# Row sums of the attention weights: four accumulating DMAs and a VectorE reduce for 28 heads, in place of a ones matmul for every two or four heads

## The chip, the cores and the metric

The kernel runs on one core of a Trainium2 chip. The core has five engines that work side by side: TensorE (PE in the profile) multiplies matrices, VectorE (DVE) and ScalarE (ACT) work on elements, GpSimd (POOL) and SyncE (SP) here mostly issue DMAs. An engine takes its instructions strictly in order, so an instruction that waits holds all that stand behind it on that engine. Transfers run on 16 DMA engines that all queues share. Accumulating DMAs, which add what they carry to what lies at the destination, are issued from POOL; most others from SP.

The metric is the device time of one execution in microseconds; of several executions the median counts.

## The reference: what is computed

```python
def _A_ref(x, wqkv, wo):                      # attention: B=1, S=2048, D=1024, H=32 heads, Dh=32
    qkv = (x @ wqkv).reshape(B, S, 3, H, Dh).transpose(2, 0, 3, 1, 4)
    q, k, v = qkv[0], qkv[1], qkv[2]
    scores = jnp.einsum("bhqd,bhkd->bhqk", q, k) * (Dh ** -0.5)
    p = _softmax(scores, axis=-1)
    o = jnp.einsum("bhqk,bhkd->bhqd", p, v)
    return o.transpose(0, 2, 1, 3).reshape(B, S, D) @ wo
...
g = _sigmoid((x * gate_w).sum(-1, keepdims=True))
a = _A_ref(x, A_wqkv, A_wo)
b = _B_ref(x, B_w_q, B_k1, B_k2, B_u, B_v)    # experts chosen by product keys
return g * a + (1 - g) * b
```

All of it is in 32-bit floats. The change concerns one quantity: for each head and each of the 2048 queries, the sum of exp(score) over the 2048 keys, by which the softmax divides.

## The kernel before

The kernel has three stages. The first projects x to queries and keys, routes to the experts and computes the values, and leaves its results in device memory. The second, from about 628 to 1625 us of the profile, is the attention of 32 heads. The third multiplies by wo, adds the experts' part and stores the output. The change lies in the second stage, apart from one constant tile that is set up at the start.

**Steps.** The attention is cut into 512 steps, 32 heads by 16 key tiles of 128 keys; step 16 h + kt is key tile kt of head h. For each step `scores` (line 1272) multiplies a key tile with all 2048 queries in four units of 512 queries. Each unit fills one bank of `ring`, seven banks of PSUM that are used in turn, and ScalarE takes the exponential of one to four banks at once (line 1294) into a tile P[h, kt] of 128 keys x 2048 queries. `pv` (line 1299) multiplies P with the values; a head's output gathers in the tile `o`, which ScalarE copies to `osb` when the head is done (`finish`, line 1407). Units come in batches of 8 to 10, and a batch's activations are cut where a key tile ends, where the ring wraps around, and after each of the first units of a batch longer than the ring.

**Row sums.** A head's 16 tiles P are added up to one tile of 128 x 2048 in two ways. In `PAIRS` stand pairs of tiles that an accumulating DMA of POOL adds into one, (0, 2), (4, 6) and (8, 10) for all heads but the last (`accumulate`, line 1335, at steps 4, 8 and 12 of the head). VectorE adds the other ten tiles into the head's accumulator ACC[h] as they come (`presum`, line 1323), and the sums of the pairs at steps 12, 17 and 21 of the head, counted on into the next head (`add_pair`, `merge4` and the like). `add` (line 1344) is two VectorE instructions of 128 x 1024.

What is left is a sum over the 128 partitions, which VectorE can't form, and so TensorE does it: with a matrix of ones, `head_sums` (line 1400) multiplies a tile into one bank of the ring, ScalarE copies the bank to `ssb` (line 1417), and SP stores the rows to SMD. To need one such matmul for four heads rather than four, the kernel folds each head of the first 24 from 128 partitions to 32 and puts it into its quarter of a shared tile T (`merge4`, `fold4`, `fold4_end`: two accumulating DMAs for the first head of four, three for the others, and for these an add of 32 partitions more on VectorE). The matrix `ones4` keeps the four quarters apart. Heads 24 to 29 are folded to 64 partitions and taken two at a time with `ones2`; heads 30 and 31 are taken alone. T lies in `rb0`, which the third stage needs for its first factors (`load_rb` from step 495 on).

For each group of four heads `load_r` then loads the sums as 128 x 64, and `norm_r` (line 1427) takes the reciprocal, multiplies it with the gate in G64 and stores it to RD, from which the third stage loads its factors.

**What sets the order.** Everything is written out by hand. `at(step, f, ...)` (line 1475) puts a call on a list for a step; the loop at line 1542 emits a batch of scores, the multiplications with values that lag behind it, and then for each finished step its listed calls and its `presum`. Each call lands at that place in the queues of the engines that it uses.

**Buffers.** `p_tile` (line 1158) chooses the place of each new P among 13 places, 11 from step 328 on and 10 from step 443 on, as the one that is free first by a fixed plan: a tile of a pair is planned for 14 or 10 steps, any other for 5. The accumulators come from two buffers named `acc` that are used in turn.

## Time and profile before

| | |
|---|---|
| median of three timed runs | 1811.02 us (1810.2 to 1812.05) |
| the profiled execution's own time | 1811.52 us |
| its span, first to last instruction | 1809.7 us |
| TensorE busy, matmuls | 1801.0 us |
| VectorE busy | 1503.6 us |
| ScalarE busy | 1221.5 us |
| GpSimd busy | 262.4 us |
| granted TensorE clock | 1.00 |

The profile is of one execution. Its page gives the busy time of each engine, the span in 40 slices (a digit is the busy share in tenths), the chain of work that ended last followed back from the end, and groups of instructions: source line, engine, operation, what is written and read, shape, count, then busy time, mean duration in nanoseconds and the idle time of the engine before them with what ended it. Matmuls overlap, so that a busy TensorE isn't TensorE at its peak, and the mean of one matmul is longer than its share of the busy time. A multiplication of plain 32-bit floats shows as two matmul records. A view by windows gives each engine's busy time in a stretch with the number of its instructions, the clock, the DMA share and the rate in GB/s.

### The profile page before, as it was taken

To read this page: it belongs to the slowest core of one execution; us is meant where nothing else is said; L and a number is where in the kernel's file an instruction comes from. 1 tells how busy PE (TensorE), PEld (TensorE's weight loads), DVE (VectorE), ACT (ScalarE), POOL (GpSimd) and SP (SyncE) were. 2 spreads that over 40 slices of the span, in tenths; PEclk is the share of its full clock that TensorE was granted. 3 is DMA by queue.
4 is the path that set the end of the run, shared out by engine and by line. 5 is a ranking of instruction groups with operands and counts; after the bars stand their busy time and mean duration, and the time that the engine had idled before them with its cause. 6 is when DMAs were issued, how large, how long until landed. Compare 5 with 4: busy or idle time off the path is not lost.

```text
span 1809.7 us, 28079 instructions
## 1 busy us (share of the span) xinstructions
PE 1801.0 (100%) x10631; PEld 1137.0 (63%) x10631; DVE 1503.6 (83%) x1673; ACT 1221.5 (67%) x1613; POOL 262.4 (15%) x314
## 2 busy tenths in 40 slices
PE   9999999999999999999999999999999999999999
PEld 7877777788888745555454555454555545547887
DVE  7868776358988689999989999999899989995674
ACT  4434321211233399999999999999999999993221
POOL 0212000026401211111211111111112010101000
PEclk9999999999999999999999999999999999999999
DMA  6887888723238699999999999999999998957851
GB/s 234 243 284 248 272 267 295 258 79 106 82 129 276 225 217 185 195 198 199 191 202 205 208 209 194 206 184 208 200 202 198 207 199 189 201 130 228 280 168 58
DMA packets 132225, 364.74 MB, mean 202 GB/s; under 512 B 17540, under 2 KB 57876, under 8 KB 106168
## 3 DMA queue, kind: packets, MB, share of 16 engines
q0 software_dynamic: 22064, 136.07, 39.3%
q1 hardware_dynamic: 89864, 190.94, 35.3%
q10 hardware_dynamic: 20160, 35.92, 7.0%
q8 instruction: 84, 1.38, 0.3%
q14 instruction: 53, 0.43, 0.1%
HBM read 169.14 MB, written 72.10 MB: 133 GB/s over the span
## 4 chain that ended last, share of the span: by engine, by line
PE 97%; DMA 2%; ACT 0%; issue 0%; DVE 0%; SPq 0%; ACTq 0%; DVEq 0%
PE ring L1285 29%; PE o L1306 26%; PE bk L157 13%; PE bk L713 10%; PE pa L157 6%; PE bk L760 5%; PE bk L928 2%; PE bk L313 2%; PE pa L1582 2%; PE bk L493 1%; PE bk L397 1%; PE pa L1589 1%; DMA wraw<-in_wqkv 1%; DMA smd<-ssb 1%; PE ring L1319 0%; ACT P L1294 0%
## 5 line engine op out<-in xcount | busy, mean ns | idle before, releaser
L1294 ACT ACTIVATE P<-ring 128x512 f32<-128x512 f32 (+3 forms) x995 | 807.8, 932 | 12.9 <-PE ring L1285 6.7
L1347 DVE TENSOR_TENSOR acc<-acc,P 128x1024 f32<-128x1024 f32 x516 | 596.0, 1219 | 30.5 <-ACT P L1294 29.8
L1306 PE MATMUL o<-P,V 128*32 128x512 f32 (+1 forms) x3896 | 408.7, 540 | 0.0
L1285 PE MATMUL ring<-Q,K 98*128 98x512 f32 x1024 | 269.4, 406 | 0.0
L1285 PE MATMUL ring<-z,z 98*128 98x512 f32 x1020 | 267.5, 406 | 0.1
L1285 PEld LDWEIGHTS ring<-Q,K 98*128 98x128 f32 x1024 | 182.7, 188 | 121.4 <-ACT P L1294 42.1
L1285 PEld LDWEIGHTS ring<-z,z 98*128 98x128 f32 x1020 | 182.1, 188 | 114.6 <-issue 39.5
L1306 PEld LDWEIGHTS o<-P,V 128*32 128x32 f32 x3896 | 108.4, 109 | 203.8 <-issue 179.7
L1336 POOL DMA_DIRECT2D P<-P x78 | 81.4, 1043 | 496.5 <-PE o L1306 190.5
L1347 DVE TENSOR_TENSOR acc<-acc,wo_raw 128x1024 f32<-128x1024 f32 x118 | 139.0, 1220 | 13.4 <-ACT wo_raw L1294 13.4
L1294 ACT ACTIVATE wo_raw<-ring 128x512 f32<-128x512 f32 (+3 forms) x134 | 119.6, 988 | 0.0
L242 ACT ACTIVATE hi<-bk 128x512 fp32r<-128x512 f32 x40 | 23.7, 594 | 116.4 <-PE bk L713 102.2
L713 PE MATMUL bk<-xh,e 128*128 128x512 f32 x384 | 94.2, 394 | 0.0
L713 PE MATMUL bk<-xl,e 128*128 128x512 f32 x384 | 92.2, 389 | 0.0
L713 PEld LDWEIGHTS bk<-xh,e 128*128 128x128 f32 x384 | 71.0, 188 | 22.0 <-issue 3.4
L1347 DVE TENSOR_TENSOR acc<-P,P 128x1024 f32<-128x1024 f32 x60 | 70.8, 1221 | 16.2 <-ACT P L1294 15.9
L255 DVE TENSOR_TENSOR lo<-bk,hi 128x512 fp32r<-128x512 f32 x40 | 27.6, 690 | 67.5 <-ACT hi L242 62.7
L713 PEld LDWEIGHTS bk<-xl,e 128*128 128x128 f32 x384 | 72.1, 188 | 15.0
L103 DVE TENSOR_TENSOR e<-wraw,e 128x512 fp32r<-128x512 f32 (+3 forms) x64 | 54.6, 861 | 27.0 <-ACT e L102 26.7
L102 ACT ACTIVATE e<-wraw 128x512 fp32r<-128x512 f32 (+3 forms) x64 | 44.7, 705 | 37.7 <-DMA wraw<-in_wqkv 22.0
L157 PE MATMUL bk<-xh,e 128*128 128x512 f32 x288 | 68.5, 393 | 0.0
L1306 PE MATMUL o<-wo_raw,V 128*32 128x256 f32 (+1 forms) x632 | 66.6, 496 | 0.0
(300 smaller groups left out, 2377.4 us busy)
## 6 DMA issues: line engine op xcount, KB each, us to landing
P<-P POOLq DMA_DIRECT2D x78, 1024.0 KB, 12.0
wqt<-in_wq SPq DMA_DIRECT2D x26, 1024.0 KB
wraw<-in_wqkv SPq DMA_DIRECT2D x30, 512.0 KB
vhl<-P POOLq DMA_DIRECT2D x13, 1024.0 KB, 13.5
rb<-acc POOLq DMA_DIRECT2D x36, 256.0 KB, 7.2
qdh<-hi ACTq DMA_DIRECT2D x32, 256.0 KB
qdl<-lo ACTq DMA_DIRECT2D x32, 256.0 KB
kdh<-hi ACTq DMA_DIRECT2D x32, 256.0 KB
```

Source lines behind the costliest of these rows:

```text
L102: nc.scalar.activation(hi, src, AF.Copy)
L103: (on or nc.vector).tensor_tensor(out=lo, in0=src, in1=hi.bitcast(F32), op=OP.subtract)
L157: nc.tensor.matmul(ps, self.a[a][i][:, k, :], self.b[b][j][k], start=(not first and k == 0 and i == j == 0), stop=(k == HC - 1 and i == 1))
L313: nc.tensor.matmul(ps[32 * quad:32 * quad + 32, :], kpad[:, quad % 2, i, :], t[:, quad, :], start=(i == 0), stop=(i == 3))
L713: nc.tensor.matmul(ps, t[:, kc // HC, a, kc % HC], x_at(b, n, kc), start=first, stop=last)
L760: nc.tensor.matmul(ps, x_at(a, t // 4, kc)[:, tok], b, start=first, stop=last)
L928: nc.tensor.matmul(p, x_at(a, t // 4, kc)[:, tok], b, start=first, stop=last)
L1285: on_ring(nc.tensor.matmul(ring[:, i, :], K[:98, kt * 128:(kt + 1) * 128], Q[:98, qc * 512:(qc + 1) * 512], start=True, stop=True), i)
L1294: on_ring(nc.scalar.activation(P[h, kt][:, q0 * 512:(q0 + m) * 512].rearrange("p (a m) -> p a m", a=m), ring[:, i:i + m, :], AF.Exp, scale ...
L1306: nc.tensor.matmul(O[h][32 * qc:32 * qc + 32, c0:c1], Vt[g][:, kt, 32 * j:32 * j + 32], p[:, qc * 512 + c0:qc * 512 + c1], start=(kt == 0) ...
L1336: nc.gpsimd.dma_start(P[h, b], P[h, a], accum_op=OP.add)
L1347: nc.vector.tensor_add(out[:, c], a[:, c], b[:, c])
```

## The change

Heads 0 to 27 go another way. Each is summed into an accumulator of its own, and four accumulating DMAs fold it from 128 partitions to 64, 32, 16 and 8. SP stores the eight rows to a new tensor SED. For each group of four heads, `load_eight` loads the 8 x 4 rows as 128 partitions of 8 x 64, and `sum_eight` adds the eight on VectorE in one reduce, whose input is read with a stride; `norm_r` follows at once. Heads 28 and 29 still share a matmul with `ones2`, now in ACC[28], and 30 and 31 are as before. T becomes the third accumulator, used for every third head, since an accumulator is now held longer. In odd heads below 28 the pair (4, 6) is gone: VectorE adds both tiles itself. `ones4` goes, and a filling tile grows by its size.

```diff
+    SED = [dram.tile([8, 4, S], F32, name=f"sed{g}") for g in range(G - 1)]
...
-    ones4 = const.tile([128, 32], F32, name="ones4")
...
-    const.tile([128, 120], F32, name="fill")
+    const.tile([128, 152], F32, name="fill")
...
-    PAIRS = ((0, 2), (4, 6), (8, 10)), ((2, 4), (2, 6))
+    def pairs_of(h):
+        if h == H - 1:
+            return (2, 4), (2, 6)
+        if h % 2 and h < H - 4:
+            return (0, 2), (8, 10)
+        return (0, 2), (4, 6), (8, 10)
...
-                ACC[h] = wk.tile([128, S], F32, name="acc")
+                ACC[h] = T if h % 3 == 2 else wk.tile([128, S], F32, name="acc")
...
     def merge_odd(h):
         add(ACC[h][up], ACC[h][up], pair(h, -1)[up])
-        add(T[low], ACC[h][low], pair(h, -1)[low])
+        add(ACC[h - 1][low], ACC[h][low], pair(h, -1)[low])
 
     def fold_odd(h):
-        nc.gpsimd.dma_start(T[low], ACC.pop(h)[up], accum_op=OP.add)
+        nc.gpsimd.dma_start(ACC[h - 1][low], ACC.pop(h)[up], accum_op=OP.add)
...
+    def fold(h, n):
+        nc.gpsimd.dma_start(ACC[h][:n], ACC[h][n:2 * n], accum_op=OP.add)
+
+    def store_eight(h):
+        g, j = divmod(h, 4)
+        dma(SED[g][:, j, :], ACC.pop(h)[:8])
...
+    def load_eight(g):
+        R[g] = wk.tile([128, 512], F32, name="ssb").rearrange("p (r m) -> p r m", m=64)
+        dma(R[g], SED[g].rearrange("r j (b m) -> (j b) r m", m=64))
+
+    def sum_eight(g):
+        r = wk.tile([128, 128], F32, name="rr", bufs=1)[:, :64]
+        nc.vector.tensor_reduce(r, R[g].rearrange("p r m -> p m r"), axis=AX.X, op=OP.add)
+        R[g] = r
...
             at(base + 12, add_pair, h, 0)
-            at(base + NT + 1, add_pair, h, 1)
+            if len(pairs_of(h)) == 3:
+                at(base + NT + 1, add_pair, h, 1)
             at(base + NT, finish, h)
+            at(base + NT + 5, merge_odd if h == H - 3 else merge, h)
             if h == H - 2:
-                at(base + NT + 5, merge, h)
                 at(base + NT + 8, head_sums, h)
-            elif g < FOURS:
-                at(base + NT + 5, merge4, h)
-                at(base + NT + 7, fold4, h)
-                at(base + NT + 11, fold4_end, h)
+            elif h == H - 3:
+                at(base + NT + 7, fold_odd, h)
+                at(base + NT + 14, head_sums, h - 1, 2)
             else:
-                at(base + NT + 5, (merge_even, merge_odd)[h % 2], h)
-                at(base + NT + 7, (fold_even, fold_odd)[h % 2], h)
-                if h % 2:
-                    at(base + NT + 14, head_sums, h - 1, 2)
+                at(base + NT + 7, fold, h, 64)
+                if g + 1 < G:
+                    at(base + NT + 12, fold, h, 32)
+                    at(base + NT + 17, fold, h, 16)
+                    at(base + NT + 21, fold, h, 8)
+                    at(base + NT + 26, store_eight, h)
         if j == 3 and g + 1 < G:
-            if g < FOURS:
-                at(base + NT + 18, head_sums, h - 3, 4)
-            at(base + NT + (24 if g < FOURS else 18), load_r, g)
-            at(base + NT + (36 if g < FOURS else 25), norm_r, g)
+            at(base + NT + 33, load_eight, g)
+            at(base + NT + 40, sum_eight, g)
+            at(base + NT + 40, norm_r, g)
```

More of the change, by code (lines that the diff above doesn't have):

```diff
@@ L70, in gated_mha_peer_kernel @@
     ones2 = const.tile([128, 32], F32, name="ones2")
[L71 to L79 removed]
+    nc.vector.memset(ones2, 0.0)
+    for i in range(2):
+        nc.vector.memset(ones2[64 * i:64 * i + 64, 16 * i:16 * i + 16], 1.0)
+    const.tile([128, 152], F32, name="fill")
     ctx.enter_context(tc.tile_pool(name="fillr", bufs=1, side="right")).tile([128, 120], F32, name="fillr")
@@ L1323, in presum @@
     def presum(h, kt):
-        pairs = PAIRS[h == H - 1]
+        pairs = pairs_of(h)
         first, second = [t for t in range(NT) if t not in sum(pairs, ())][:2]
@@ L1482, in gated_mha_peer_kernel @@
             at(base - 1, load_head, h + 1)
-        for b, a in PAIRS[h == H - 1]:
+        for b, a in pairs_of(h):
             at(base + b + 4, accumulate, h, b, a)
```

41 lines of the change are left out of this document (3 added, 38 removed).

## The prediction, made before the changed kernel was run

> **What bounds the kernel now.** I read the page first. Its span is the profiled execution's own; that execution took 1811.5 us on the device, 1.8 us more than the span and 0.5 us more than the median of the three timed runs (1811.0).
>
> ```profile
> span 1809.7 us, 28079 instructions
> ...
> PE 1801.0 (100%) x10631; PEld 1137.0 (63%) x10631; DVE 1503.6 (83%) x1673; ACT 1221.5 (67%) x1613; POOL 262.4 (15%) x314
> ...
> DMA  6887888723238699999999999999999998957851
> ...
> q0 software_dynamic: 22064, 136.07, 39.3%
> ...
> PE ring L1285 29%; PE o L1306 26%; PE bk L157 13%; PE bk L713 10%; PE pa L157 6%; PE bk L760 5%; PE bk L928 2%; PE bk L313 2%; PE pa L1582 2%; PE bk L493 1%; PE bk L397 1%; PE pa L1589 1%; DMA wraw<-in_wqkv 1%; DMA smd<-ssb 1%; PE ring L1319 0%; ACT P L1294 0%
> ```
>
> The chain that ends last is TensorE nearly throughout; attention (scores into ring, values into o) is over half of it. In that stage DMA is also near full, so four resources have to be looked at, not one. The averages do not say which of them sets the pace, so I cut the stage by heads: the windows below run from one evacuation of a head's output (osb, line 1410) to the next. I show the shortest and the longest window without a ones matmul (217 matmul records), then all nine that hold one (225).
>
> ```profile
> core 0: us, PE busy (x) PEld busy (x) DVE busy (x) ACT busy (x) POOL busy (x), PEclk, DMA share, GB/s
> ...
> 1003.93:1034.87 30.94, 30.94 (x217) 15.64 (x218) 29.95 (x27) 30.50 (x39) 5.06 (x6) 1.00 1.00 205
> 1378.49:1409.50 31.01, 31.01 (x217) 15.61 (x218) 29.79 (x27) 30.53 (x40) 5.07 (x6) 1.00 1.01 200
> ...
> 785.17:817.13 31.96, 31.96 (x225) 15.93 (x226) 27.77 (x26) 31.15 (x41) 4.27 (x5) 1.00 1.01 210
> 910.05:942.00 31.95, 31.95 (x225) 15.94 (x226) 27.55 (x25) 31.00 (x42) 4.28 (x5) 1.00 1.01 201
> 1034.87:1066.81 31.94, 31.94 (x225) 15.86 (x226) 27.62 (x25) 31.00 (x40) 4.25 (x5) 1.00 1.04 224
> 1159.75:1191.70 31.95, 31.95 (x225) 15.91 (x226) 27.81 (x26) 31.06 (x39) 4.28 (x5) 1.00 1.02 210
> 1284.62:1316.59 31.97, 31.97 (x225) 15.95 (x226) 27.57 (x25) 31.05 (x43) 4.25 (x5) 1.00 1.01 217
> 1409.50:1441.43 31.93, 31.93 (x225) 15.90 (x226) 27.64 (x25) 30.93 (x40) 3.44 (x4) 1.00 1.01 219
> 1441.43:1473.37 31.94, 31.94 (x225) 16.03 (x226) 31.38 (x29) 31.18 (x42) 3.46 (x4) 1.00 0.82 180
> 1504.33:1536.18 31.85, 31.85 (x225) 16.00 (x226) 30.83 (x27) 30.99 (x38) 3.46 (x4) 1.00 0.82 180
> 1567.15:1599.04 31.89, 31.89 (x225) 16.01 (x226) 30.73 (x27) 31.04 (x41) 3.46 (x4) 1.00 0.75 160
> ```
>
> A head takes 30.97 us or, with one ones matmul, 31.9. Nothing else moves it: not VectorE (27.5 to 31.4 us busy), not the DMA share (0.75 to 1.04). TensorE and ScalarE are the pair that sets the pace (ScalarE is busy 30.5 of 30.94), and the granted clock is 1.00 throughout. A step, one key tile of a head, is 30.97 / 16 = 1.94 us. The waits of ScalarE between 660 and 1625 us confirm it; these three are all:
>
> ```profile
> ACT P L1294 <- PE ring L1285: 5.1, 26, 0.3
> ACT ssb L1417 <- PE ring L1319: 5.0, 10, 0.7
> ACT vhl L1294 <- PE ring L1285: 1.2, 6, 0.3
> ```
>
> ScalarE never waits for a P buffer, so neither VectorE's adds nor the accumulating DMAs, which free those buffers, are ever late enough to count.
>
> **The ones matmuls that go.** The chain around the first of the nine, and a batch of ten scores that follows no such matmul:
>
> ```profile
> 787.39 2.29 PE o L1306 x24
> 789.68 0.86 PE ring L1319 x8
> 790.54 2.71 PE ring L1285 x10
> ...
> 821.62 2.60 PE ring L1285 x10
> ```
>
> The matmul adds 0.86 us to the chain, and the next batch takes 0.11 longer: 0.97. By lines, with the rows that the other terms need:
>
> ```profile
> L1319 PE MATMUL ring<-rb,ones 128*32 128x512 f32 x72 | 9.4, 592 | 0.0
> L1417 ACT ACTIVATE ssb<-ring 128x512 f32<-128x512 f32 x10 | 6.0, 599 | 5.0 <-PE ring L1319 5.0
> L1294 ACT ACTIVATE P<-ring 128x512 f32<-128x512 f32 x607 | 336.4, 630 | 10.8 <-PE ring L1285 5.1
> L1294 ACT ACTIVATE P<-ring 128x1024 f32<-128x1024 f32 x155 | 160.5, 1075 | 0.0
> L1347 DVE TENSOR_TENSOR acc<-acc,P 128x1024 f32<-128x1024 f32 x499 | 576.1, 1219 | 27.2 <-ACT P L1294 26.4
> L1347 DVE TENSOR_TENSOR rb<-acc,P 32x1024 f32<-32x1024 f32 x18 | 21.2, 1213 | 0.3
> L781 DVE TENSOR_REDUCE mm<-eq 128x64 f32<-128x512 f32 x16 | 10.9, 684 | 7.7 <-POOL eq L774 7.7
> ```
>
> Nine matmuls of eight records are 9.4 us, 1.04 each on TensorE; the copies of the sums (line 1417) are 6.0 + 5.0 us for ten, 1.10 each on ScalarE with its wait. Both engines lose about the same, which is why the windows show it whole. The ninth window's matmul (heads 28 and 29) stays. The first eight windows add up to 255.49 us; less 8 x 30.97 = 247.76 that is **7.7 us** removed. The bounds are 8 x 0.86 = 6.9 (the chain's matmuls alone) and 8 x 1.10 = 8.8.
>
> **The scores' batches.** Each head_sums takes one bank of the ring of seven, so without eight of them the later batches start on other banks, and scores() cuts its activations where the ring wraps. Following its rule batch by batch gives 1189 activations before, which is the page's count (995 + 134 + 60), and 1192 after. One more cut turns a 1075 ns activation into two of 630, 0.19 us: 0.6 us at most on ScalarE, nothing if TensorE is the later. I take +0.1.
>
> **VectorE.** One add() is two instructions of 576.1 / 499 = 1.155 us, so 2.31; on 32 partitions it costs the same (21.2 / 18). Removed: the second add of merge4 in 18 heads and of merge_odd in heads 25 and 27, 20 adds. Added: 14 odd heads add tiles 4 and 6 separately in presum instead of their sum once, 14 adds; and seven sum_eight. The reduce of L781 has just its shape, 0.68 us, though its input is contiguous and the new one is strided; doubled it would be 1.4. Net -20 x 2.31 + 14 x 2.31 + 7 x 0.68 = -9.1 us of work that was covered: no term. The cover does get uneven. From one odd head's first step to the next head's come 14 adds (32.3 us, more than a head), over an even head's 11 (25.4). So VectorE falls 1.4 us behind in odd heads and recovers in the even ones; that is the third rival.
>
> **DMA and its queues.** POOL's issues go from 167 to 195: 14 pair accumulations fewer, 42 folds more. The bytes: 14 MB less from pairs; folds go from 24 x 768 KB + 4 x 512 KB (20 MB) to 28 x 960 KB (26.3 MB); stores and loads of eight rows add 28 x 128 KB (3.5 MB). Some 4 MB less, over a stage that is full: no gain counted, no loss. The new risk is waiting in order.
>
> ```profile
> P<-P POOLq DMA_DIRECT2D x78, 1024.0 KB, 12.0
> vhl<-P POOLq DMA_DIRECT2D x13, 1024.0 KB, 13.5
> rb<-acc POOLq DMA_DIRECT2D x36, 256.0 KB, 7.2
> rb<-rb POOLq DMA_DIRECT2D x9, 512.0 KB, 9.0
> L1398 POOL DMA_DIRECT2D rb<-acc x18 | 14.1, 781 | 119.3 <-DMA rb<-acc 66.1 <-PE ring L1285 53.3
> SPq L84 <- DMA smd<-ssb: 73.0, 11, 14.3
> ```
>
> Fold 64 is issued at step 23, 32 at 28, 16 at 33, 8 at 37, the store on SP at 42: gaps of 5, 5, 4 and 5 steps, 9.7 and 7.7 us. The first lands in about 9.0 (the 512 KB row), the 256 KB one in 7.2, the two smaller ones, which no row shows, between nothing and 7.2; I take 7.2. Each is down before the next is issued, by 0.5 us at the tightest. If one is late, POOL waits and the pair accumulation (8, 10) behind it starts late; its sum lands 12 to 13.5 us after step 12, or at step 19, and merge wants it at step 21 of the head, about 3 us of cover. POOL waits so already (66.1 us at line 1398) at no cost. On SP the store waits for fold 8 ahead of load_wo, load_head and the store of osb; load_head runs a whole head ahead, and SP already waits up to 14.3 us for smd. load_eight comes 7 steps before sum_eight (13.6 us); that load has 1024 pieces of 256 bytes where load_r has 128, and lateness there would hold VectorE. The accumulator is written again three heads later at step 51, nine steps (17 us) after its store. The last group's reciprocals reach RD at step 488 instead of 473, seven steps before load_rb reads them. All of it: 0.
>
> The Trainium skill (DMA: Bandwidth & Descriptors, Bandwidth, measured table) says to batch DMAs to at least 1 MiB and calls transfers under 64 KB descriptor-dominated; the change goes the other way, down to that size. Its fit of 2.0 us plus bytes over 436 GB/s (same page, Anatomy of one DMA) would make the four folds 3.2 + 2.6 + 2.3 + 2.2 us, and the sum would stay as it is; the trace's 9.0 and 7.2 are three times that, and the trace decides.
>
> **Sum.** -7.7 + 0.1 = -7.6 us: the profiled execution 1803.9, the median 1811.0 - 7.6 = **1803.4 us**. Its own range: 8.8 less gives 1802.2; 6.9 less, the whole 0.6 for cuts and 1 us of buffer waits in the last four heads, where P has ten places for thirteen, gives 1805.7.
>
> **Rivals.**
> Half the gain: ScalarE alone sets the pace and closes the holes, so that only the copy itself (line 1417, 0.60 each) is saved, 8 x 0.60 = 4.8, less 0.6 for cuts: 1806.8. For it: ScalarE is 98% busy. Against: the windows show 0.97.
> Slower by the folds: a late fold 64 holds POOL, the accumulation (8, 10) behind it, merge, the P buffers and then ScalarE. It decides when fold 64 lands later than 9.7 + 3 = 12.7 us; at 13.5, as the 1 MB rows do at worst in the median, 0.8 us in each of 28 heads is 22 us lost, 1811.0 - 7.6 + 22 = 1825. For it: DMA is full in the stage, and even heads move more than before (3 MB and 960 KB). Against: 512 KB lands in 9.0 today, odd heads move 0.8 MB less, and VectorE can make up some 2 us a head. The skill's batching rule, above, speaks for this one.
> Slower by VectorE: the 1.4 us backlog of 14 odd heads reaches ScalarE through the P buffers, 20 us: 1823. It decides once a buffer is wanted sooner than VectorE's backlog allows. Against: the planner hands out fewer tiles for long in odd heads, and VectorE waits for ScalarE today (26.4 us).
> Nothing left: the last heads' waits and small ones give back 4.1 or more of the 7.6: 1808 to 1812.
>
> **Chances.** Forecast 0.70, half the gain 0.12, nothing left 0.08, folds 0.06, VectorE 0.04. A measurement here tells 0.2%, 3.6 us, from no change. Faster: the first two, less a little, 0.81; same 0.09; slower 0.10. The range 1800.5 to 1808.5 holds the first two, and below them as much as the runs differ (1.8 us).
>
> **What would show it.** Right: no 225-record windows but one, 30.97 us for all heads, odd and even; line 1319 down to 8 ring records; ScalarE's waits still on TensorE alone; line 1347 with six adds (12 instructions) fewer; folds landing under 9.7 us. Wrong: ScalarE waiting for VectorE or a DMA at line 1294; VectorE idle before sum_eight for a load, or before a merge for an accumulation; heads of 32 us and more by parity.

## The result: 5% slower, and the profile after

| | before | after |
|---|---|---|
| median of six runs each, us | 1810.61 (1809.88 to 1812.05) | 1908.93 (1897.24 to 1936.28) |
| ratio, 95% interval | | 1.0526 [1.0487, 1.0565] |
| profiled execution, its own time | 1811.52 | 1905.18 |
| up to the first osb, us | 661.3 | 660.5 |
| attention, first osb to last | 967.7 | 1045.2 |
| third stage, last osb to the end | 180.8 | 197.7 |

The slowest run of after, 1936.28 us, counts as slow and is not in the ratio, which compares means and not medians. The forecast of 1803.4 us was wrong, in sign and in size. The profiled executions differ by 93.7 us: 77.5 in the attention, 16.9 in the third stage, which the change does not touch, and -0.8 ahead of them.

The page of after, the lines that answer to those of before:

```profile
span 1903.4 us, 28032 instructions
...
PE 1822.2 (96%) x10567; PEld 1142.5 (60%) x10567; DVE 1490.8 (78%) x1663; ACT 1219.1 (64%) x1608; POOL 285.3 (15%) x342
...
PEclk9999999999999999999989989989989999999999
DMA  7788988630277889997998999889989989747772
...
q0 software_dynamic: 21744, 127.94, 35.8%
...
PE 74%; DMA 15%; DVE 4%; issue 3%; ACT 3%; SPq 1%; ACTq 0%; DVEq 0%
```

TensorE executes 64 matmul records fewer (the eight ones matmuls) and VectorE and ScalarE are busy for less time, yet TensorE is no longer busy throughout, its granted clock has notches at a regular distance, and transfers are 15% of the chain that ends last. The windows of after, by heads as in the prediction, show what the notches are. Of 31 windows here are a quiet one, the first disturbed pair, two later ones and the sum:

```profile
784.43:815.39 30.96, 30.96 (x217) 15.67 (x218) 26.89 (x25) 30.60 (x41) 4.83 (x6) 1.00 0.86 169
815.39:858.07 42.68, 32.45 (x222) 16.57 (x222) 24.51 (x24) 30.71 (x40) 6.70 (x8) 0.93 0.92 190
858.07:891.62 33.55, 33.21 (x211) 15.53 (x212) 33.55 (x31) 30.46 (x38) 5.07 (x6) 0.89 0.62 123
...
1490.67:1532.43 41.76, 32.72 (x217) 16.11 (x218) 25.09 (x24) 30.88 (x41) 5.91 (x7) 0.88 1.00 202
...
1626.60:1674.71 48.11, 35.45 (x220) 16.11 (x220) 28.77 (x27) 31.26 (x41) 3.46 (x4) 0.82 0.67 136
...
sum 1045.20, PE 984.38 PEld 487.97 DVE 897.64 ACT 945.90 POOL 162.00; mean PE 31.75 PEld 15.74 DVE 28.96 ACT 30.51 POOL 5.23
```

A head without a disturbance takes 30.96 us, as forecast. One head in four takes 37.6 to 48.1 us, seven times: once for each group of four heads, at the place of `sum_eight`. After the first four of these the next head takes 33.0 to 33.6 us at a granted clock of 0.89 to 0.91: the clock stays lower for a while after the stall. Who waited, by the waits of the whole execution (engine, line, for whom: us in total, times, longest):

```profile
POOL acc L1368 <- DMA acc<-acc: 227.8, 35, 12.5
...
DVE rr L1406 <- DMA ssb<-sed: 101.2, 7, 17.1
...
POOL rb L1368 <- DMA rb<-rb: 91.3, 15, 11.6
...
ACT P L1298 <- DVE acc L1351: 52.3, 7, 12.2
...
DVE V L1618 <- DMA P<-rd: 33.9, 4, 13.8
...
ACT P L1298 <- DVE rb L1351: 16.1, 2, 9.6
```

VectorE waits seven times for `load_eight`, ScalarE then for VectorE's accumulators, which before it never did. In order of time around the first of the seven, from the timelines of SP, VectorE and ScalarE (start, duration; in brackets the idle time ahead and its releaser):

```profile
816.08 0.52 SPq L82 DMA_DIRECT2D od<-osb  x1
816.65 0.97 SPq L82 DMA_DIRECT2D ssb<-sed  x1
817.66 18.97 SPq L82 DMA_DIRECT2D V<-vd  x1
850.69 0.34 SPq L82 DMA_DIRECT2D rd<-rr  x1
...
827.07 4.63 DVE L1351 TENSOR_TENSOR acc<-acc,P 128x1024 f32<-128x1024 f32 x4
848.81 1.01 DVE L1406 TENSOR_REDUCE rr<-ssb 128x64 f32<-128x512 f32 x1 [17.11 <-DMA ssb<-sed]
...
840.33 5.62 ACT L1298 ACTIVATE P<-ring 128x512 f32<-128x512 f32 x6
857.57 0.60 ACT L1298 ACTIVATE P<-ring 128x512 f32<-128x512 f32 x1 [11.62 <-DVE acc L1351]
```

The load is issued at 816.65 and VectorE can start its reduce at 848.81, 32.2 us later; the schedule gave it 13.6. VectorE stands still for 17.1 us; all adds behind it, and the buffers that they free, are late; ScalarE stands still for 11.6 us, and with it the scores. In the seven groups the time from issue to reduce is 32.2, 26.8, 27.1, 23.9, 26.2, 23.7 and 23.6 us.

The folds land later than the prediction took them, and nearly independent of their size (issues in after: count, KB each, median us to landing):

```profile
acc<-acc POOLq DMA_DIRECT2D x20, 512.0 KB, 10.7
...
acc<-acc POOLq DMA_DIRECT2D x19, 256.0 KB, 7.7
...
acc<-acc POOLq DMA_DIRECT2D x19, 128.0 KB, 9.6
...
acc<-acc POOLq DMA_DIRECT2D x19, 64.0 KB, 9.9
```

The third stage does the same instructions with the same transfers; here it is by windows in before and then in after:

```profile
1628.90:1809.70 180.80, 175.81 (x786) 143.01 (x784) 110.49 (x161) 43.92 (x71) 8.43 (x15) 1.00 0.59 184
```

```profile
1705.70:1903.40 197.70, 180.35 (x784) 145.45 (x784) 111.27 (x162) 43.69 (x71) 8.44 (x15) 0.96 0.62 168
```

The rate falls from 184 to 168 GB/s. Of the some 22,870 packets of this stage 14,080 are of 1 KB, in both kernels, most of them reads of OD and RD. By the trace's record of each packet one takes 60.0 ns in the mean before and 74.3 after; the median is 46 in both, so that only a part of them became much slower.

### The profile page after: what moved, and what is told of

The parts are those of the page before. It is cut to its first block, busy times and chain, and to the rows that moved or that the text cites. A ratio compares the mean times of both kernels' runs of the same rounds, so it can differ in the third digit from the quotient of the medians.

```text
span 1903.4 us, 28032 instructions
## 1 busy us (share of the span) xinstructions
PE 1822.2 (96%) x10567; PEld 1142.5 (60%) x10567; DVE 1490.8 (78%) x1663; ACT 1219.1 (64%) x1608; POOL 285.3 (15%) x342
## 4 chain that ended last, share of the span: by engine, by line
PE 74%; DMA 15%; DVE 4%; issue 3%; ACT 3%; SPq 1%; ACTq 0%; DVEq 0%
PE ring L1289 19%; PE o L1310 17%; PE bk L155 12%; DMA ssb<-sed 10%; PE bk L711 9%; PE bk L758 5%; PE pa L155 4%; ACT P L1298 3%; PE bk L926 2%; DVE acc L1351 2%; DMA od<-osb 2%; PE bk L311 2%; PE bk L491 1%; DMA wo_raw<-t1l 1%; PE pa L1565 1%
## 5 line engine op out<-in xcount | busy, mean ns | idle before, releaser
L1351 DVE TENSOR_TENSOR acc<-acc,P 128x1024 f32<-128x1024 f32 x414 | 477.1, 1226 | 14.6 <-ACT P L1298 10.4
L1310 PE MATMUL o<-P,V 128*32 128x512 f32 (+1 forms) x4024 | 429.3, 547 | 0.0
L1289 PE MATMUL ring<-Q,K 98*128 98x512 f32 x1024 | 279.0, 415 | 60.3 <-ACT P L1298 60.3
L1351 DVE TENSOR_TENSOR rb<-rb,P 128x1024 f32<-128x1024 f32 x186 | 214.8, 1224 | 3.5 <-ACT P L1298 3.4
L1368 POOL DMA_DIRECT2D acc<-acc x77 | 64.0, 831 | 392.2 <-DMA acc<-acc 227.8
L1340 POOL DMA_DIRECT2D P<-P x60 | 60.9, 1015 | 269.4 <-ACT P L1298 87.2
L1298 ACT ACTIVATE wo_raw<-ring 128x512 f32<-128x512 f32 (+3 forms) x110 | 100.0, 979 | 1.7 <-PE ring L1289 1.3
L240 ACT ACTIVATE hi<-bk 128x512 fp32r<-128x512 f32 x40 | 23.7, 595 | 113.0 <-PE bk L711 91.9
L711 PE MATMUL bk<-xh,e 128*128 128x512 f32 x384 | 94.2, 394 | 0.0
L1406 DVE TENSOR_REDUCE rr<-ssb 128x64 f32<-128x512 f32 x7 | 7.4, 1051 | 101.2 <-DMA ssb<-sed 101.2
L1351 DVE TENSOR_TENSOR acc<-acc,wo_raw 128x1024 f32<-128x1024 f32 x56 | 66.0, 1227 | 9.7 <-DMA wo_raw<-P 7.0
L1298 ACT ACTIVATE vhl<-ring 128x512 f32<-128x512 f32 (+3 forms) x83 | 70.9, 937 | 0.2
## 6 DMA issues: line engine op xcount, KB each, us to landing
acc<-acc POOLq DMA_DIRECT2D x20, 512.0 KB, 10.7
```

The lines of the kernel that those rows point to most:

```text
L711: nc.tensor.matmul(ps, t[:, kc // HC, a, kc % HC], x_at(b, n, kc), start=first, stop=last)
L1289: on_ring(nc.tensor.matmul(ring[:, i, :], K[:98, kt * 128:(kt + 1) * 128], Q[:98, qc * 512:(qc + 1) * 512], start=True, stop=True), i)
L1298: on_ring(nc.scalar.activation(P[h, kt][:, q0 * 512:(q0 + m) * 512].rearrange("p (a m) -> p a m", a=m), ring[:, i:i + m, :], AF.Exp, scale ...
L1310: nc.tensor.matmul(O[h][32 * qc:32 * qc + 32, c0:c1], Vt[g][:, kt, 32 * j:32 * j + 32], p[:, qc * 512 + c0:qc * 512 + c1], start=(kt == 0) ...
L1340: nc.gpsimd.dma_start(P[h, b], P[h, a], accum_op=OP.add)
L1351: nc.vector.tensor_add(out[:, c], a[:, c], b[:, c])
```

## The experiments

The theory was that the attention loses by the load of the eight rows; its rival, that it loses by the folds. The third stage, and a VectorE without slack, got theories of their own. Each kernel is the changed one with the edit shown, unless said otherwise. In the diffs `...` stands for changed lines that are not shown. The letters of the theories (A to D) are those of each expectation and change their meaning between them. All results first; the last two columns are of one profiled execution.

| kernel | median, us | ratio to before, 95% | attention | third stage |
|---|---|---|---|---|
| no_load | 1833.64 | 1.0137 [1.0120, 1.0154] | 960.0 | 197.1 |
| pool_load | 1840.12 | 1.0165 [1.0146, 1.0184] | 975.7 | 197.2 |
| pieces_in_store | 1892.71 | 1.0417 [1.0363, 1.0470] | 1038.7 | 197.0 |
| later_sum | 1837.13 | 1.0116 [1.0065, 1.0167] | 994.5 | 186.0 |
| to_four | 1919.65 | 1.0594 [1.0557, 1.0631] | 1068.9 | 191.2 |
| early_load | 1849.06 | 1.0246 [1.0190, 1.0301] | 982.3 | 200.7 |
| early_pieces | 1848.43 | 1.0183 [1.0138, 1.0229] | 989.4 | 196.6 |
| head_later | 1933.28 | 1.0677 [1.0638, 1.0715] | 1068.0 | 197.2 |
| before_pad | 1824.28 | 1.0068 [1.0046, 1.0091] | 967.7 | 193.4 |
| after_place | 1904.99 | 1.0539 [1.0487, 1.0590] | 1029.9 | 182.0 |
| pool_place | 1825.17 | 1.0076 [1.0037, 1.0115] | 982.8 | 181.8 |
| no_load_place | 1827.38 | 1.0112 [1.0077, 1.0147] | 970.4 | 183.7 |
| no_load_pitch | 1836.34 | 1.0155 [1.0115, 1.0196] | 972.1 | 196.4 |
| pool_pitch | 1835.46 | 1.0140 [1.0096, 1.0184] | 972.7 | 195.9 |
| pairs_alone | 1816.08 | 1.0020 [1.0003, 1.0036] | 968.3 | 184.1 |
| spaced_place | 1829.37 | 1.0104 [1.0087, 1.0122] | 982.2 | 183.6 |
| sixteen_place | 1815.87 | 1.0033 [1.0015, 1.0051] | 961.0 | 186.7 |
| sixteen_three | 1893.52 | 1.0445 [1.0398, 1.0493] | 1046.6 | 181.7 |

### Is it the load?

**no_load** leaves the load out; VectorE sets the eight rows to one, so that the sums of 28 heads are not computed.

```diff
-        dma(R[g], SED[g].rearrange("r j (b m) -> (j b) r m", m=64))
+        nc.vector.memset(R[g], 1.0)
```

> The changed kernel without the load of the eight rows: VectorE fills the tile with ones (0.3 us or so) where the load stood, so the sums of 28 heads are left out; all folds, stores and the reduce stay. Theory A (the load of 1024 pieces of 256 bytes lands too late, 32 us after its issue where 13.6 were allowed, and VectorE stands still for it 101 us in all): no windows of 37 to 48 us are left, every head takes 31.0, and the attention from the first to the last osb falls from 1045 to about 960 us; total 1803 to 1806 if the third stage's 17 us came with it, 1820 if they did not. Theory B (the chain of four folds and a full DMA make everything late, and the load is only where it shows): most of the loss stays, above 1850.

The windows of no_load, the one at the place of the first stall, the only one that holds a ones matmul, and the sum:

```profile
815.69:846.64 30.95, 30.95 (x217) 15.67 (x218) 30.82 (x30) 30.59 (x39) 5.95 (x7) 1.00 1.01 196
...
1559.10:1590.99 31.89, 31.89 (x225) 16.03 (x226) 31.70 (x30) 31.07 (x40) 3.47 (x4) 1.00 0.85 183
...
sum 960.04, PE 960.04 PEld 483.00 DVE 897.74 ACT 944.61 POOL 162.27; mean PE 30.97 PEld 15.58 DVE 28.96 ACT 30.47 POOL 5.23
```

The attention takes 960.0 us, 7.7 less than before: the forecast gain, in full, and 85 us less than after. The load is the first cause. But this profiled execution is by luck the fastest of its kernel (1819.6 of 1819.6 to 1838.9). The median is 1833.64, 30 above the forecast, since the third stage is as slow as in after and the attention, it seems, longer in other executions: two more kernels without the load, described below, took 970.4 and 972.1 us in it. So the load is worth 73 to 85 us.

**pool_load** issues the same load from POOL.

```diff
-        dma(R[g], SED[g].rearrange("r j (b m) -> (j b) r m", m=64))
+        dma(R[g], SED[g].rearrange("r j (b m) -> (j b) r m", m=64), nc.gpsimd)
```

> The changed kernel with the same load of 256-byte pieces, issued from POOL's queue instead of SP's, so that its pieces stand in one queue with the accumulating DMAs and not against them. Theory A with turns (two queues take turns piece by piece on a DMA engine, 256 bytes against 8 KB): in one queue 64 small pieces of an engine follow each other at some 20 ns, the load lands in 8 to 13 us, VectorE hardly waits: 1803 to 1808. Theory A without turns (1024 pieces are slow in themselves): as slow as before, 1890 to 1910. Theory B: above 1850.

It lands 13.7 us after its issue in the median, VectorE does not wait for it, and 69 us are back (1840.12). But more differs than the queue. From the two profile pages, after and then pool_load:

```profile
DMA packets 138403, 359.85 MB, mean 189 GB/s; under 512 B 24596, under 2 KB 64932, under 8 KB 113112
```

```profile
DMA packets 131683, 359.85 MB, mean 196 GB/s; under 512 B 17428, under 2 KB 57764, under 8 KB 106392
```

There are 7168 packets under 512 B fewer, seven loads of 1024: on POOL's queue each load is recorded as 64 packets of 4 KB, though the instruction still names 256-byte pieces. The first load is also issued 4.9 us sooner (811.73 instead of 816.65), since on SP it stands behind K, Q and the store of osb. So the bytes of the load do not make it late. Its way through SP's queue does, by its pieces, its place there, or both.

### Its pieces, or its place in the queue?

**pieces_in_store** lays SED out so that the load has 128 pieces of 2 KB, and the stores the 256-byte pieces.

```diff
-    SED = [dram.tile([8, 4, S], F32, name=f"sed{g}") for g in range(G - 1)]
+    SED = [dram.tile([4, 32, 8, 64], F32, name=f"sed{g}") for g in range(G - 1)]
...
```

> The changed kernel with the small pieces moved from the load to the stores: SED is laid out so that the load has 128 pieces of 2 KB (8 for each engine), and each of four stores has 256 pieces of 256 bytes (32 for each of eight engines), with two heads to go until its accumulator is written again. Theory A: the load lands within 10 us of its issue, but a store can take 32 turns of 0.63 us, 20 us, against 13.6 until the load and 17 until the accumulator is used again: VectorE waits 0 to 7 us in a group, total 1803 to 1850. If the number of pieces of the load does not matter: 1890 to 1910.

VectorE still waits 80.2 us for the load and the median is 1892.71: an eighth of the pieces, and the time from issue to reduce is 25.4 us in the mean against 26.2.

**to_four** adds a fifth fold, to four rows, so that the load has half the pieces and half the bytes.

```diff
...
-        dma(SED[g][:, j, :], ACC.pop(h)[:8])
+        dma(SED[g][:, j, :], ACC.pop(h)[:4])
...
+                    at(base + NT + 24, fold, h, 4)
```

> The changed kernel with a fifth fold to four rows, 3 steps after the fourth, so that the load on SP's queue has 512 pieces of 256 bytes instead of 1024 (32 instead of 64 for each engine) and the reduce adds four rows; nothing else is changed. Theory A with turns: the load takes half as long, 16 instead of 32 us, VectorE waits some 2 to 4 us in a group instead of 14.5, the attention falls from 1045 to 965 to 990 us, third stage still about 197, total 1825 to 1850. Rival (a fixed latency of the load, or the chain of folds): 1890 to 1920.

1919.65, slower than after. From issue to reduce it is 21.9 us in the mean, not half of 26.2, and the load starts later: the store that it depends on waits in SP's queue for one more fold. SP's own wait for folds of `acc` goes from 196.8 to 268.3 us, and in the first group the store leaves at 817.4 instead of 804.9 and the load at 830.2 instead of 816.7. VectorE's wait comes to 108.5 us. By these two runs the count of pieces alone is not the cause.

**later_sum** gives the load time: the reduce comes 16 steps later (the last group 6).

```diff
-            at(base + NT + 40, sum_eight, g)
-            at(base + NT + 40, norm_r, g)
+            at(base + NT + (46 if g + 2 == G else 56), sum_eight, g)
+            at(base + NT + (46 if g + 2 == G else 56), norm_r, g)
```

> The changed kernel with the reduce and norm_r 16 steps (31 us) later, the load where it was; for the last group 6 steps later, the most that load_rb allows. Theory A: the load, 32 us after its issue, is down before VectorE comes to the reduce at 45 us; six of seven waits vanish, the last shrinks from 15 to about 4 us: 1805 to 1825. Theory B: above 1850.

VectorE's wait for ssb falls to 5.2 us and 72 us are back. New is a wait of VectorE for the stores of the rows before it may overwrite an accumulator (25.4 us for acc, 8.9 for rb).

**early_load** moves the load ahead of the K and Q loads of a later head, and leaves the reduce where it is. **early_pieces** is pieces_in_store with the same edit.

```diff
-            at(base + NT + 33, load_eight, g)
+            at(base + NT + 29, load_eight, g)
```

> Changed kernel with one difference: load_eight is called at step NT + 29 instead of NT + 33, so that it stands in SP's queue ahead of load_head's eight loads (K, Q; step NT + 31) and not behind them; sum_eight stays at NT + 40. Theory A (the load is late because its pieces stand behind about 1.75 MB of K and Q on the same queue): the load lands about 10 us after its issue, VectorE's wait for ssb falls from 101 us to under 25, the attention stage from 1045 to 975 to 990 us, the total to 1840 to 1860 (the third stage keeps its 13 to 17 us). Theory B (1024 pieces of 256 bytes that take turns with 8 KB pieces, 64 per DMA engine by 0.63 us = 40 us at worst): issue to reduce stays at 25 us and more, so that moving it by four steps (7.7 us) takes 7 x 7.7 = 54 us off at most, the wait stays over 40 us and the total over 1865.

> pieces_in_store (2 KB pieces in the load, 256-byte pieces in the four stores) with the load at step NT + 29, ahead of load_head's loads. Theory A: as early_load, within 10 us of it, since only the place in the queue counts: 1840 to 1860. Theory B: the piece count counts, so this one alone is cured: at least 20 us faster than early_load. If both counts hold (place and pieces), early_load lies half way and this one at 1830 to 1845.

VectorE no longer waits for the load in either, and they are alike (1849.06 and 1848.43): with the place right, 1024 pieces are no worse than 128. The numbers are those that theory A (the place in SP's queue) had forecast: attention 982.3 and median 1849. SP's timeline of early_load, around the first load:

```profile
806.21 0.28 SPq L82 DMA_DIRECT2D sed<-acc  x1
812.64 0.39 SPq L82 DMA_DIRECT2D ssb<-sed  x1
813.12 2.29 SPq L82 DMA_DIRECT2D K<-kdh  x2
...
826.26 0.52 SPq L82 DMA_DIRECT2D od<-osb  x1
```

By the records of single pieces, the load's last piece is down 12.3, 9.1, 8.9, 9.6, 10.4, 8.9 and 5.8 us after the issue, 9.3 in the mean; in after the mean is 25.7. How the pieces go, in counts per microsecond, from the same records:

```
after       SP 256 B  POOL 8 KB        early_load  SP 256 B  POOL 8 KB
823 to 824    498        13            815 to 816     15        30
826 to 827      4        27            818 to 819     29        27
836 to 837      1        21            820 to 821     94         3
847 to 848    107         0            821 to 822    723         4
```

When POOL's stream of accumulating 8 KB pieces pauses, hundreds of the small pieces go in a microsecond. When it flows, from 815 to 820 in early_load 108 small pieces go and 123 of POOL's: one for one, so that each 256 bytes wait for 8 KB. In after's first group half of the pieces are down 7.1 us after the issue; the rest take another 24 us. Ten of the 16 DMA engines count the load's semaphore up by 824.65 and the last one at 848.79. The records do not name the engine of a piece, but this fits a load that waits for the few engines on which POOL's stream does not pause. The Trainium skill (DMA: Bandwidth & Descriptors, Queues, rings and completion order) says that each DMA engine takes turns between the queues that have work for it. The trace agrees with the turns. The same section of the Trainium skill has, as typical, 9 to 17 descriptors go from one queue before the next has its turn. Equal counts like 108 and 123 would fit that too, if both queues had turns of the same length; but from 832.62 to 837.74 in after the small pieces start one at a time, 0.63 to 0.64 us apart but for one that falls in between, and an 8 KB piece of POOL takes 0.63 us in the median of the attention. These are turns of one.

**head_later** keeps the load's step and moves only the K and Q loads, three steps, behind it.

```diff
-            at(base - 1, load_head, h + 1)
+            at(base + 2, load_head, h + 1)
```

> Changed kernel with one difference: load_head's eight loads of K and Q are issued three steps later (behind load_eight instead of ahead of it); the load keeps its step NT + 33 and its time. Theory A (K and Q ahead of it on SP's queue make it late): it now lands about 10 us after its issue as in early_load (9.3 us there, 25.7 in the changed kernel), VectorE's wait for it falls under 25 us, total 1840 to 1860. Theory C (what counts is when it meets POOL's stream of 8 KB accumulating pieces, with which its 256-byte pieces take turns; early_load only moved it into a pause of that stream): it still lands 20 us and more after its issue, VectorE waits over 60 us, total over 1880.

Neither theory's total came: 1933.28. The load is down 7.4, 27.8, 11.7, 27.1, 9.4, 7.3 and 7.2 us after its issue, in five groups of seven as theory A has it and in two as theory C, and VectorE waits three times. But the delay went to another place, as the waits of VectorE and then of TensorE show:

```profile
DVE rr L1406 <- DMA ssb<-sed: 32.6, 3, 16.2
```

```profile
PE ring L1289 <- DMA z<-shd: 30.6, 7, 5.3
PE ring L1289 <- DMA Q<-shd: 12.9, 1, 12.9
PE ring L1289 <- DMA Q<-qdh: 11.2, 1, 11.2
```

TensorE waits for K and Q, which it did in no head of before: they have no three steps to spare. This slows the whole stage, and so moves the load against POOL's stream as well. What follows is that the load is late by what stands around it on SP's queue and on POOL's; how much of it is K and Q ahead of it and how much the meeting with POOL's stream is not settled, since both moves shift both.

### The third stage

**before_pad** is the kernel before, with nothing changed but the room for SMD, 32 KB, made 256 KB each.

```diff
-    SMD = [dram.tile([4, S], F32, name=f"smd{g}") for g in range(G)]
+    SMD = [dram.tile([32, S], F32, name=f"smd{g}")[:4] for g in range(G)]
```

> The kernel before, with nothing changed but the size of the eight SMD tensors in device memory: 256 KB each where 32 KB are used, so that the outputs of the head groups (OD), which lie between them, stand 1 MB + 256 KB apart from the third group on, as in the changed kernel, where they stood 1 MB + 32 KB apart. Theory C (the third stage's 17 us come from where OD and RD lie in device memory: their 1 KB reads took 79 ns on average without the load of the eight rows and 60 ns before): attention as before (967.7 us from the first to the last osb), third stage 195 to 198 us instead of 180.7, total 1825 to 1829. Rival (the third stage is late because the end of the attention leaves its queues late): no change, 1811.

```profile
661.30:1629.00 967.70, 967.64 (x6744) 485.32 (x6745) 910.54 (x805) 948.53 (x1196) 139.28 (x164) 1.00 0.96 196
1629.00:1822.40 193.40, 180.68 (x784) 145.76 (x784) 110.08 (x161) 43.53 (x71) 8.45 (x15) 0.97 0.65 172
```

The attention is that of before to the tenth, the third stage is 12.6 us longer at 172 GB/s, a 1 KB read takes 77.7 ns, and the four runs lie within 1.1 us. No instruction and no transfer differs; only addresses do. By the addresses that the built kernels have, the OD tensors, 1 MB each, start from the third on 1 MB and 32 KB apart in before, with an SMD between each two (two SMDs ahead of the last); in after the 256 KB of an SED come between and no SMD for 28 heads.

**after_place** is after with the addresses of before: SED in the space of a tensor that is no longer needed (WPD), and 128 bytes stored to each SMD so that it keeps its place.

```diff
+    SED = WPD.rearrange("p k m -> (p k m)").rearrange("(g r j s) -> g r j s", g=G - 1, r=8, j=4)
...
+    def touch(g):
+        dma(SMD[g][0:1, 0:32], ones[0:1, :])
...
```

> The changed kernel with every tensor of device memory back where it lay in the kernel before: SED takes the space of WPD, which is no longer used by then, and 128 bytes are stored to each SMD tensor so that it keeps its place between the OD tensors. Theory C (place in device memory): third stage 181 us instead of 197.7, attention still 1045 us as after, total 1885 to 1895. Rival (the third stage is late because of the late attention): 1900 to 1915 as after.

```profile
1690.20:1872.20 182.00, 175.73 (x784) 142.94 (x784) 111.67 (x162) 43.90 (x71) 8.43 (x15) 1.00 0.58 183
```

183 GB/s, 60.0 ns a read and 182.0 us: the third stage of before. The median hardly shows it (1904.99), because the attention varies by more from execution to execution. pool_load and **pool_place**, which has both cures, show it cleanly: third stage 197.2 and 181.8, medians 1840.12 and 1825.17.

> Both cures: the load of the eight rows on POOL's queue, and the old places in device memory. Theories A with turns and C: attention 960 to 976 us, third stage 181, total 1803 to 1822. If the folds' waits in POOL's queue are a third cause, the upper half of that with attention windows over 31 us late in the stage; if not, 1803 to 1806.

Two more tried another distance, 288 KB instead of 256, by four more rows in SED: **no_load_pitch** (like no_load, without the load) and **pool_pitch** (like pool_load).

> The changed kernel without the load of the eight rows (as no_load: the sums of 28 heads are left out), with each SED tensor padded from 256 to 288 KB, so that the OD tensors stand 1 MB + 288 KB apart. Theory C: if the distance modulo 256 KB decides, the third stage is back at about 181 us and the total at 1803 to 1805, the forecast; if only the old distance of 32 KB helps, 1815 to 1836 as no_load. Rival: as no_load.

> The changed kernel with the load of the eight rows on POOL's queue (as pool_load, 1836 to 1843) and the SED tensors padded to 288 KB. Theory C: 16 us less than pool_load, 1820 to 1827; its attention of 975.7 us stays. Rival: as pool_load.

Their third stages take 196.4 and 195.9 us: no cure. In to_four, whose SED tensors have 128 KB, it takes 191.2 us at 74.5 ns a read. So where the tensors lie counts, and not the distance of 256 KB alone; which places are good, and why, no run shows. The price also varies: later_sum has after's distances between the OD tensors and lost only some 5 us (186.0, at 70.3 ns a read).

### What is left

**pairs_alone** is before with only two pairs in the odd heads below 28, the part of the change that loads VectorE.

> The kernel before with the other part of the change alone: odd heads below 28 have two pairs added by DMA instead of three, VectorE adds the tiles 4 and 6 itself; ones matmuls, folds to 32 partitions and T as before. VectorE then has 14 adds of 2.31 us in an odd head's 31.0 us (32.3) and about 12.5 in an even one. Theory: buffers cover it, attention 967 to 972 us, total 1811 to 1816. Rival (VectorE's load in odd heads stops ScalarE): 1.4 us lost in each of 14 heads, 1830 or more.

1816.08, attention 968.3: the backlog in odd heads does not reach ScalarE. In the profiled execution, 3.3 us are lost in the third stage (184.1), for which no run gives the cause.

**no_load_place** has neither the load nor the new addresses; again the sums of 28 heads are left out.

> The load of the eight rows left out (VectorE sets them to one, so that the sums of 28 heads are wrong) and the device memory laid out as in the kernel before (SED in the space of another tensor, 128 bytes stored to each SMD). If the load and the places are the two causes and nothing else is lost: attention 960, third stage 181, total 1803 to 1806, the forecast. If the folds in POOL's queue cost as well: attention 965 to 975, total 1808 to 1820, with POOL waiting over 300 us for folds.

The attention took 970.4 us and the median is 1827.38, in the range for folds that cost as well, and above it. With both causes gone, the median is still some 24 us above the forecast. The waits of POOL and VectorE in pool_place, which has the same folds:

```profile
POOL acc L1368 <- DMA acc<-acc: 272.8, 36, 11.6
POOL rb L1368 <- DMA rb<-rb: 149.6, 19, 11.8
...
DVE acc L1351 <- DMA P<-P: 29.3, 8, 6.1
```

A fold that has not landed holds POOL; the pair accumulation behind it is issued late, and VectorE waits for its sum.

**spaced_place** is pool_place with the four folds 6, 7 and 6 steps apart, the store five steps later, the load three and the reduce four.

```diff
-                    at(base + NT + 12, fold, h, 32)
-                    at(base + NT + 17, fold, h, 16)
-                    at(base + NT + 21, fold, h, 8)
-                    at(base + NT + 26, store_eight, h)
+                    at(base + NT + 13, fold, h, 32)
+                    at(base + NT + 20, fold, h, 16)
+                    at(base + NT + 26, fold, h, 8)
+                    at(base + NT + 31, store_eight, h)
...
-            at(base + NT + 33, load_eight, g)
-            at(base + NT + 40, sum_eight, g)
-            at(base + NT + 40, norm_r, g)
...
+            at(base + NT + 36, load_eight, g)
+            at(base + NT + 44, sum_eight, g)
+            at(base + NT + 44, norm_r, g)
```

> pool_place with the four folds at steps NT + 7, 13, 20, 26 instead of 7, 12, 17, 21 (store at 31, load at 36, reduce at 44). If the folds cost because each is issued before the one before has landed (about 10 us, 5 steps): POOL's waits for folds fall from 422 us to under 100, attention from 983 to 960 to 968, total 1805 to 1815, as with three folds. If the fourth fold itself is what costs (POOL and the DMA engines have too much to do): no better than pool_place, 1820 to 1830.

```profile
POOL acc L1368 <- DMA acc<-acc: 152.6, 24, 15.5
...
POOL rb L1368 <- DMA rb<-rb: 72.2, 10, 16.3
...
DVE acc L1351 <- DMA wpd<-acc: 33.2, 7, 7.8
```

POOL's waits halve, VectorE's for the pairs go (29.3 to 1.2 us), and a wait for the later store, which holds the accumulator, takes their place. 1829.37: no better.

**sixteen_place** is pool_place with three folds, to 16 rows, at steps 7, 13 and 21; the load comes in two halves on POOL and VectorE reduces both and adds.

```diff
...
-                    at(base + NT + 12, fold, h, 32)
-                    at(base + NT + 17, fold, h, 16)
-                    at(base + NT + 21, fold, h, 8)
-                    at(base + NT + 26, store_eight, h)
+                    at(base + NT + 13, fold, h, 32)
+                    at(base + NT + 21, fold, h, 16)
+                    at(base + NT + 27, store_eight, h)
...
```

> As pool_place, but each head is folded only to 16 rows by three DMAs, with 6 and 8 steps between them instead of 5, 5 and 4, and each behind the pair accumulation next to it; 16 rows are stored, loaded on POOL's queue in two DMAs of 1024 pieces, and summed by two reduces and a small add. Theory D (a fold that isn't down yet holds POOL and the pair accumulations behind it): POOL's waits for folds (about 455 us in pool_load) fall to under 100 us, the windows are all 31 us, total 1803 to 1806, below pool_place. Rival (the doubled load costs more): at or above pool_place, 1806 to 1825.

```profile
POOL acc L1368 <- DMA acc<-acc: 8.6, 9, 1.5
POOL rb L1368 <- DMA rb<-rb: 7.6, 6, 3.1
```

POOL's waits for folds go from 422 to 16 us and the attention to 961.0, the forecast's. The profiled execution took 1809.29, the median of ten is 1815.87 (1809.3 to 1826.8), with 186.7 us in the third stage. The median is 9 us below pool_place's, though the intervals of the two overlap; more of the folds' cost is not shown. It is still 12 us above the forecast, and for that no run gives the cause; pairs_alone by itself is 5 us above before. sixteen_place is the best version of the change that was run, and at 1.0033 [1.0015, 1.0051] it is still not faster than before.

**sixteen_three** is sixteen_place with three pairs in all heads, 14 accumulations of 1 MB more.

> sixteen_place with three pairs in every head, as in the kernel before (VectorE 14 adds fewer, POOL 14 accumulations of 1 MB more). If two pairs in the odd heads cost what pairs_alone lost (5 us) by leaving VectorE no slack: attention 961 or less, 1808 to 1812 in the median and runs closer together than sixteen_place's 1809 to 1827. If the DMA engines are what is short: POOL waits longer for folds, 1816 to 1830.

```profile
POOL acc L1366 <- DMA acc<-acc: 194.1, 26, 12.9
...
DVE acc L1349 <- DMA qdh<-acc: 73.7, 10, 13.4
DVE rb L1349 <- DMA qdh<-rb: 37.5, 3, 15.6
```

1893.52: the direction of the rival (the DMA engines are short) at several times its price. Folds are late again, so are the stores, and VectorE waits 111 us for accumulators. The two pairs in odd heads make the room that the folds need.

## Why the prediction was wrong, point by point

- **The ones matmuls, -7.7 us: right.** In no_load 29 windows of 31 take 30.92 to 31.09 us, one has 225 records and 31.89 us, the last is short, and the attention is 7.7 us shorter (967.7 to 960.0). The rival of half the gain falls.
- **Cuts of the ring: right.** 999 + 110 + 83 = 1192 activations in after.
- **VectorE, no term: right in effect.** `add` executes 12 instructions fewer (808 to 796), and pairs_alone, at 1816.08 where the rival by backlog asks for 1823 and more, rules this rival out. The strided reduce takes 1051 ns, between the 0.68 us taken and the 1.4 named.
- **"load_eight comes 7 steps before sum_eight (13.6 us) ... All of it: 0": this step failed, and it decided.** The risk was named and priced at nothing, with no duration for the load: it takes 23.3 to 31.3 us to its last piece. No rival carried it either: the chance of 0.10 for slower stood on the folds and on VectorE's backlog. What could have warned is the order of SP's queue: load_r stood ahead of the next load_head's K and Q and had twelve steps to norm_r, while load_eight stands right behind them and behind the store of osb, and has seven. Worth 73 to 85 us of attention in the profiled executions (1045.2 against 972.1, 970.4 and 960.0 without the load).
- **The folds, "each is down before the next is issued": failed.** The two small ones, taken at 7.2 us, take 9.6 to 10.8, longer than the 256 KB one; the gaps are 9.7 and 7.7. POOL's waits for folds go to 319 us in after. What it costs is smaller and varies: with the folds as they are the attention without the load took 960.0 us in one execution and 970.4 in another (no_load_place), and 9 us of median, hardly clear of noise, came back when sixteen_place took the waits away. The rival had the mechanism but put it on fold 64 (12.7 us; it landed in 10.7), not on the small ones.
- **The third stage was not looked at.** A new tensor moved the others: 12.6 us by before_pad, 15 us by pool_load and pool_place, 5 us in later_sum.
- **Nothing else of note:** POOL's 28 issues more are there (314 to 342 instructions), and its bytes fall by 8 MB, as counted.

So the forecast gain is real and three costs bury it: the load (some 70 to 85 us), the addresses (mostly 13 to 17) and the folds in POOL's order (some 9, hardly clear of noise). What stays open: the share of K and Q in the load's delay, the some 12 us that sixteen_place's median lies above the forecast (6 of them in the third stage of its profiled execution), and why the runs of most kernels with the four folds scatter by 14 us and more, where all runs of before but three (1817.7, 1822.0 and 1826.0) lie within 3.

## What to carry to other kernels

A small load on a busy queue is late by what stands ahead of it and by the stream that it shares the DMA engines with, more than by its size: price it by issue to last piece, in its place in the queue, and give it the lead that its predecessor had. An engine that waits in order for a small result passes the wait on to all that is queued behind it; put the consumer far behind the load or the load ahead of the bulk. And compare the addresses of all tensors after adding one: a stage that the change does not touch can lose more than the change was to gain.

## What the hardware did that was not expected

- Accumulating folds of 64 KB land in 9.9 us and those of 512 KB in 10.7 (after): in a full stage the size hardly counts.
- SP's issue of the next transfer behind the late load (V<-vd at 817.66) took 18.97 us, and 12.9 to 22.1 us in five of the seven groups, where such an issue takes 0.5 in the median. In pieces_in_store, whose load has an eighth of the pieces, none of them took 3 us.
- The same load of 1024 pieces of 256 bytes is recorded as 1024 packets on SP's queue (after) and as 64 packets of 4 KB on POOL's (pool_load).
- On a DMA engine where both queues have work, one 256-byte piece of SP goes for one 8 KB piece of POOL, every 0.63 to 0.64 us (after, 832.62 to 837.74).
- Where the 1 MB tensors lie in device memory moves the mean of the 1 KB reads from 60 to 78 ns (before against before_pad).
- After stalls of TensorE of 5 to 10 us the granted clock of the following head is 0.89 to 0.91 four times, and it takes 33 us instead of 31: part of a stall's price is paid after it.
